# Transposes of one sequence's k and q tiles in one run on TensorE, and a lower rank for the sums of weights, in a scheduled attention and channel-mix kernel

## The chip, the cores and the metric

The kernel runs on one core of a Trainium2 chip. The metric is the device time in microseconds of one execution, median of three runs. TensorE multiplies matrices (PE in the profile; its weight loads have a row of their own, PEld), VectorE is DVE, ScalarE is ACT, GpSimd is POOL, and SyncE (SP) issues most of the DMAs.

## The reference

Eight sequences of 576 tokens, 8 heads of 64, go through an attention by way of 32 packed vectors; what comes out goes, token by token, through a channel mix with a squared relu and a sigmoid gate. All is float32.

```python
def sm_attn(qq, kk, vv):
    s = scale * np.matmul(qq, kk.transpose(0, 1, 3, 2))
    a = np.exp(s - np.max(s, axis=-1, keepdims=True))
    return np.matmul(a / (np.sum(a, axis=-1, keepdims=True) + 1e-09), vv)
p_packed = sm_attn(p, k, v)             # p: 32 vectors a head
x = sm_attn(q, p_packed, p_packed)      # heads side by side: (8, 576, 512)
xk = mu_k * x + (1 - mu_k) * x_prev     # x_prev: x one token earlier
xr = mu_r * x + (1 - mu_r) * x_prev
v = np.maximum(xk @ w_k, 0) ** 2 @ w_v  # w_k 512 x 1024, w_v 1024 x 512
out = v / (1 + np.exp(-(xr @ w_r)))     # w_r 512 x 512
```

## The kernel before

**The channel mix.** The 4608 tokens are cut into nine blocks of 512. Each operand of its matmuls is split into a high and a low part, so that a product is three matmuls of 512 columns (a triple below): `gates` (lines 1209 to 1211, 16 triples a block), `keys` (1160 to 1162, 32 triples) and `values` (1239 to 1241, 32 triples). Seven blocks go that way, and the last two go together as a pair, by a scheme of block products with fewer multiplications (Strassen's) that wants sums of blocks of the weights. Those sums are made by `sums` while blocks 2 to 6 run: adds on VectorE (line 1520), a copy on ScalarE (1496), a subtraction on VectorE (1498), and two stores to DRAM on SP's queue (`far_wr`, `far_wv`, `far_wk`); GpSimd's queue fetches them back for the pair.

**The attention.** A sequence b passes through `front` (scores of the packed vectors, line 670, the softmax `weights_of` with its exponential on line 774, their product with the values, lines 704 or 712), then `back` (scores of q, line 839, softmax, product, line 896). k and q must lie with the head dimension across partitions. For sequences 2 to 7 VectorE transposes them in blocks (line 464), and the softmax weights go to DRAM and back for their own transposition (`far<-at` and `aTd<-far`). The second sequence, b = 1, uses `transposed_on_pe`: its four k tiles and four q tiles, each six pieces of 96 tokens, are transposed on TensorE (line 479) into a PSUM slot of the pool `pa` (two slots) and copied out by ScalarE (line 482). While this happens TensorE also does the gates and keys of block 0, whose inputs come out of `first_mix` (line 1029), through the same two `pa` slots, by way of `first_out` and `first_low` (ScalarE lines 1045 and 1048, VectorE line 1054), and the weights are converted in between (`convert`: lines 299 and 311 on ScalarE, 301, 303 and 313 on VectorE).

**What sets the order.** Every piece of work is a generator that says which engine it wants next and how long that should take. `Flow.run` plays all of them against a clock of its own and emits the instructions in the order in which this planner would start them; on the chip each engine then takes its instructions strictly in that order and waits on semaphores. Of the parts that could start, the planner takes the earliest, and among equals the lowest rank:

```python
part = min(self.parts, key=self.order)
...
return start, part.rank, part.n
```

A part of sequence b ≥ 2 has rank 30 + 0.2 b in `front`, about 29 + 0.2 b in `back`. The sums of weights have `RANK_SUMS`. All names of this paragraph are planning only: no duration of the planner is a time on the chip.

Of the kernel before, what the change touches and what calls it, by code (L numbers as in the profile page):

```python
# [173 lines left out]
def attn_pack_channel_mix(ctx: ExitStack, tc: tile.TileContext, q, k, v, p, mu_k, mu_r, w_k, w_v, w_r, out):  # L174
# [31 lines left out]
    def act(n, after=None, table=None):  # L206
        return "scalar", 0.14 + 0.72e-3 * n, after, table
# [4 lines left out]
    def pe(us, after=None):  # L212
        return "tensor", us, after, None
# [20 lines left out]
    def reached():  # L234

        yield None, 0.0, None, None
# [13 lines left out]
    def tile_(shape, dtype, tag, slot, name=None):  # L250
        return sb.tile(shape, dtype, name=name or tag, tag=f"{tag}{slot}")

    def banks(slot):
        return ps.tile([P, 2, 512], F32, name="pa", tag=f"pa{slot}")
# [71 lines left out]
    def loads(b):  # L326
        flow.spawn(packed(b), lrank(b) - 0.03)
        for src, tag in ((k, "kT"), (v, "vt"), (q, "qT")):
# [8 lines left out]
            for pr in range(NPR):  # L337

                slot = yield from flow.take("raw")
                if b < EARLY:  # L340

                    raw = tile_([P, 6, 2 * D], F32, "raw", slot, "raw")
                    for hh in range(2):
                        yield from load(
                            raw[:T6, :, hh * D:(hh + 1) * D], src[b, 2 * pr + hh].rearrange("(c p) d -> p c d", p=T6),
                            0.5, 0.62,
                        )
                        back_to_issue()
                    flow.spawn(transposed_on_pe(tag, b, pr, slot, raw), rank(b), flow.free["dma"] + LANDS)
                    continue  # L350

                raw = tile_([P, NTB, 32], F32, "raw", slot)
                for o in range(0, P, 32):
                    hh, dh = divmod(o // 32, 2)
                    yield from load(
                        raw[o:o + 32],
                        src[b, 2 * pr + hh, :, 32 * dh:32 * dh + 32].rearrange("(t tb) d -> t tb d", tb=NTB),
                        0.63, 0.41,
                    )
                    back_to_issue()  # L360
                flow.spawn(transposed(tag, b, pr, slot, raw), rank(b), flow.free["dma"] + LANDS)
# [107 lines left out]
    def transposed_on_pe(tag, b, pr, raw_slot, raw):  # L469

        yield from reached()
        kq = yield from flow.take("kq")
        t = tile_([P, S], F32, "kq", kq, tag)
        slot = yield from flow.take("pa")
        pT = banks(slot)
        for hf in range(2):
            yield pe(0.25)
            for c in range(3):
                nc.tensor.transpose(pT[:, hf, c * T6:(c + 1) * T6], raw[:T6, 3 * hf + c], ident[:T6, :T6])
        flow.give("raw", raw_slot)  # L480
        yield act(S)
        nc.scalar.copy(t.rearrange("p (a b) -> p a b", a=2), pT[:, :, :HS])
        flow.give("pa", slot)
        ts[tag, b, pr] = kq, t
        flow.set((tag, b, pr))
# [704 lines left out]
    def gates(i):  # L1190

        for tiles in ((0,), (1, 2, 3)) if i == 0 else ((0, 1), (2, 3)) if i == 1 else ((t,) for t in range(NT)):
            slots, prs = [], []
            if i == 0:
                yield from flow.wait(*made("xr", i, 0, tiles[0]))
                if tiles[0]:
                    flow.keep_busy = 0.0
                    flow.give("m", 3)
            for x in tiles:
                slots.append((yield from flow.take("m")))  # L1200
                prs.append(ps.tile([P, DM], F32, name="pr", tag=f"m{slots[-1]}"))
            for c in range(NC):
                for x, pr in zip(tiles, prs):
                    ts_ = slice(x * P, (x + 1) * P)
                    yield from flow.wait(*made("xr", i, c, x), *(("wr", c, o) for o in range(0, DM, WP)))
                    yield pe(0.685)
                    flow.now.t -= flow.LAG
                    _, xh, xl = xrs[i, c]
                    nc.tensor.matmul(pr, xh[:, ts_], wr_h[:, c, :], start=(c == 0), stop=False)  # L1209
                    nc.tensor.matmul(pr, xh[:, ts_], wr_l[:, c, :], start=False, stop=False)  # L1210
                    nc.tensor.matmul(pr, xl[:, ts_], wr_h[:, c, :], start=False, stop=(c == NC - 1))  # L1211
                    if x == NT - 1:
                        flow.give("sq", xrs.pop((i, c))[0])
            for x, slot, pr in zip(tiles, slots, prs):
                flow.spawn(gated(i, x, slot, pr), 0, flow.t + flow.LAG)
# [50 lines left out]
    def channel_mix():  # L1266
        for i in range(NB - 2):
            if i == 0:
                flow.spawn(first_mix(), RANK_MIX)
            for what, u in SUMS.get(i, ()):  # L1270
                flow.spawn(sums(what, u), RANK_SUMS)
            yield from gates(i)
# [181 lines left out]

    DH = DM // 2
    FORMS = T4, T3, T2, T1
    RANK_SUMS = 20
    SUMS = {
        2: (("wr", 0), ("wr", 1)), 3: (("wv", 0), ("wv", 1)), 4: (("wv", 2), ("wv", 3)), 5: (("wk", 0),), 6: (("wk", 1),),
    }  # L1460
# [583 lines left out]
```

## Time and profile before

| | |
|---|---|
| median of 3 runs (lowest, highest) | 573.69 us (573.64, 574.53) |
| the profiled execution, its own time | 574.06 us |
| its span, first to last instruction | 572.3 us |
| granted TensorE clock, mean | 0.999 |
| TensorE busy | 564.1 us, 99% |
| VectorE busy | 444.5 us, 78% |
| ScalarE busy | 354.0 us, 62% |
| DMA, mean | 136 GB/s |

A busy TensorE is not a TensorE at its peak, since matmuls overlap: a matmul of 512 columns is shown as some 390 ns long, and the next one starts some 230 ns after it. What a wait costs on that engine is therefore read from the distance of the starts, not from the idle time alone.

### The profile page before, as it was taken

The numbers are of one execution on the slowest core, as the hardware profiler recorded it, in microseconds if no ns is written. First come the engines' busy times: TensorE is split into PE (matmuls) and PEld (weight loads), VectorE is DVE, ScalarE is ACT, GpSimd is POOL, SyncE is SP. The second block draws the span as 40 slices with busy tenths as digits, with TensorE's granted clock in tenths as the row PEclk, the third lists the DMA queues.
The fourth block names the chain that finished last, engine by engine and source line by source line (L and its number), as shares of the span: only waits on it lengthen the run. The fifth ranks groups of instructions, "written<-read, shape, count | busy, mean of one in ns | idle before, by whom it ended". The sixth has DMA issues, their size and how long they took to land.

```text
span 572.3 us, 10765 instructions
## 1 busy us (share of the span) xinstructions
PE 564.1 (99%) x4053; PEld 445.1 (78%) x4053; DVE 444.5 (78%) x815; ACT 354.0 (62%) x626; POOL 25.7 (4%) x63
## 2 busy tenths in 40 slices
PE   7999999999999999999999999999999999999997
PEld 7877777887787777778777877787778888888885
DVE  1898897929986888967897789757887579457895
ACT  4789956536924874576545675655678656377840
POOL 3000000000000000000000000000010006300000
PEclk9999999999999999999999999999999999999999
DMA  8979426760768664296339633870045019910026
GB/s 298 390 190 317 95 35 131 152 124 12 153 160 229 133 136 79 97 262 146 56 103 259 144 53 79 190 222 1 1 149 166 0 52 328 296 42 1 0 37 111
DMA packets 188884, 77.66 MB, mean 136 GB/s; under 512 B 152344, under 2 KB 173984, under 8 KB 188576
## 3 DMA queue, kind: packets, MB, share of 16 engines
q1 hardware_dynamic: 182912, 66.35, 44.8%
q0 software_dynamic: 5920, 10.62, 6.5%
q8 instruction: 32, 0.52, 0.4%
q14 instruction: 20, 0.16, 0.1%
HBM read 53.48 MB, written 23.46 MB: 134 GB/s over the span
## 4 chain that ended last, share of the span: by engine, by line
PE 92%; DMA 2%; ACT 2%; DVE 2%; issue 1%; SPq 0%; DVEq 0%; ACTq 0%
PE ph L1160 10%; PE pvo L1239 9%; PE pvo L1240 9%; PE pvo L1241 9%; PE ph L1161 9%; PE ph L1162 9%; PE pr L1209 4%; PE pr L1210 4%; PE pr L1211 4%; PE pa L704 2%; PE pa L896 2%; PE pv L1938 2%; PE pv L1940 2%; PE pv L1939 2%; PE pa L670 1%; DMA q<-in_q 1%
## 5 line engine op out<-in xcount | busy, mean ns | idle before, releaser
L1160 PE MATMUL ph<-xk,wk_h 128*128 128x512 f32 x224 | 90.3, 403 | 0.0
L1239 PE MATMUL pvo<-wv,sq 128*128 128x512 f32 x224 | 89.3, 399 | 0.0
L1161 PE MATMUL ph<-xk,wk_h 128*128 128x512 f32 x224 | 87.4, 390 | 0.0
L1162 PE MATMUL ph<-xk,wk_l 128*128 128x512 f32 x224 | 87.4, 390 | 0.0
L1240 PE MATMUL pvo<-wv,sq 128*128 128x512 f32 x224 | 87.4, 390 | 0.0
L1241 PE MATMUL pvo<-wv,sq 128*128 128x512 f32 x224 | 87.2, 389 | 0.0
L1172 ACT ACTIVATE r<-ph 128x512 f32<-128x512 f32 x56 | 33.5, 600 | 52.0 <-PE ph L1162 51.8
L1239 PEld LDWEIGHTS pvo<-wv,sq 128*128 128x128 f32 x224 | 42.1, 188 | 14.4 <-issue 5.8
L1160 PEld LDWEIGHTS ph<-xk,wk_h 128*128 128x128 f32 x224 | 42.0, 188 | 14.3 <-issue 5.9
L1162 PEld LDWEIGHTS ph<-xk,wk_l 128*128 128x128 f32 x224 | 42.0, 188 | 9.1
L1241 PEld LDWEIGHTS pvo<-wv,sq 128*128 128x128 f32 x224 | 42.1, 188 | 9.0
L1070 ACT COPY xt<-pa 128x576 f32<-128x576 f32 x28 | 30.5, 1177 | 29.7 <-PE pa L896 29.5
L1240 PEld LDWEIGHTS pvo<-wv,sq 128*128 128x128 f32 x224 | 42.1, 188 | 8.0
L1161 PEld LDWEIGHTS ph<-xk,wk_h 128*128 128x128 f32 x224 | 42.1, 188 | 7.7
L1209 PE MATMUL pr<-wr_h,xr 128*128 128x512 f32 x112 | 44.8, 400 | 0.0
L1211 PE MATMUL pr<-wr_h,xr 128*128 128x512 f32 x112 | 43.7, 390 | 0.0
L1210 PE MATMUL pr<-wr_l,xr 128*128 128x512 f32 x112 | 43.7, 390 | 0.0
L1115 DVE SCALAR_TENSOR_TENSOR x<-xt,mus,x 128x128 f32<-128x128 f32 (+5 forms) x88 | 39.8, 494 | 3.9 <-ACT x L1109 3.8
L1183 DVE CAST sq<-r 128x512 fp32r<-128x512 f32 x48 | 20.0, 417 | 29.3 <-ACT r L1175 28.3
L1185 DVE TENSOR_TENSOR sq<-r,sq 128x512 fp32r<-128x512 f32 x56 | 38.1, 681 | 5.6 <-ACT sq L1180 4.6
L1109 ACT ACTIVATE x<-xt,mus 128x128 f32<-128x128 f32 (+5 forms) x88 | 41.3, 515 | 0.7 <-DVE sq L1185 0.7
L1175 ACT ACTIVATE r<-r 128x512 f32<-128x512 f32 x56 | 35.3, 633 | 1.1
(288 smaller groups left out, 1097.5 us busy)
## 6 DMA issues: line engine op xcount, KB each, us to landing
vt<-in_v SPq DMA_DIRECT2D x14, 512.0 KB, 4.6
raw<-in_k SPq DMA_DIRECT2D x96, 72.0 KB, 2.7
raw<-in_q SPq DMA_DIRECT2D x96, 72.0 KB, 2.8
out<-sig SPq DMA_DIRECT2D x23, 256.0 KB, 3.4
st<-in_moe_w_k SPq DMA_DIRECT2D x8, 512.0 KB, 8.6
st<-in_moe_w_v SPq DMA_DIRECT2D x8, 512.0 KB, 6.6
far<-at SPq DMA_DIRECT2D x12, 288.0 KB, 2.7
aTd<-far SPq DMA_DIRECT2D x12, 256.0 KB, 3.1
```

Of the source, the lines that this page charges most:

```text
L1109: nc.scalar.mul(x32[:, o:o + n], xts[b, c][:, 1 + s:1 + s + n], mus[:, j, c:c + 1])
L1115: nc.vector.scalar_tensor_tensor(x32[:, o:o + n], xts[b, c][:, s:s + n], mus[:, j + 1, c:c + 1], x32[:, o:o + n], op0=ALU.mult, op1=ALU.add,)
L1160: nc.tensor.matmul(ph, wk_h[:, c, fs], xh, start=(c == 0), stop=False)
L1161: nc.tensor.matmul(ph, wk_h[:, c, fs], xl, start=False, stop=False)
L1162: nc.tensor.matmul(ph, wk_l[:, c, fs], xh, start=False, stop=(c == NC - 1))
L1185: nc.vector.tensor_tensor(hl[:, 1, :], r, hl[:, 0, :].bitcast(F32), op=ALU.subtract)
L1209: nc.tensor.matmul(pr, xh[:, ts_], wr_h[:, c, :], start=(c == 0), stop=False)
L1210: nc.tensor.matmul(pr, xh[:, ts_], wr_l[:, c, :], start=False, stop=False)
L1211: nc.tensor.matmul(pr, xl[:, ts_], wr_h[:, c, :], start=False, stop=(c == NC - 1))
L1239: nc.tensor.matmul(pv[t], sh, wvs[f][:, 0, :], start=(f == 0), stop=False)
L1240: nc.tensor.matmul(pv[t], sh, wvs[f][:, 1, :], start=False, stop=False)
L1241: nc.tensor.matmul(pv[t], sl, wvs[f][:, 0, :], start=False, stop=(f == NF - 1))
```

## The change

Two edits. In `transposed_on_pe` the request for TensorE is made once for all six pieces of a tile instead of once for each half of three, so that nothing can be put between the halves (and the planner counts 0.45 for the six instead of twice 0.25). And `RANK_SUMS` goes from 20 to 40, from ahead of the attention of sequences 2 to 7 to behind it.

```diff
@@ -473,8 +473,8 @@
         t = tile_([P, S], F32, "kq", kq, tag)
         slot = yield from flow.take("pa")
         pT = banks(slot)
+        yield pe(0.45)
         for hf in range(2):
-            yield pe(0.25)
             for c in range(3):
                 nc.tensor.transpose(pT[:, hf, c * T6:(c + 1) * T6], raw[:T6, 3 * hf + c], ident[:T6, :T6])
         flow.give("raw", raw_slot)
@@ -1454,7 +1454,7 @@
 
     DH = DM // 2
     FORMS = T4, T3, T2, T1
-    RANK_SUMS = 20
+    RANK_SUMS = 40
     SUMS = {
         2: (("wr", 0), ("wr", 1)), 3: (("wv", 0), ("wv", 1)), 4: (("wv", 2), ("wv", 3)), 5: (("wk", 0),), 6: (("wk", 1),),
     }
```

Every engine runs the same instructions as before, but for two loads of ScalarE's function table, of which there are 16 instead of 18. The order is the same, row for row, ahead of the first transposes of sequence 1, and again for all matmuls of the pair at the end; in between it moves on every engine. Triples and the stretches of other work between them keep their number, except that the 48 transposes of line 479 stand in 8 stretches instead of 12. The places of lines 670 to 896 among the triples are the same for sequences 2 and 3 (within five triples), and from 21 triples earlier to 15 later for sequences 4 to 7.

On TensorE, where the gates of block 0 end and its keys begin, before (`raw` is a loaded tile, `pa` the PSUM slot):

```order
L1209 MATMUL pr<-wr_h,xr 128x512
L1210 MATMUL pr<-wr_l,xr 128x512
L1211 MATMUL pr<-wr_h,xr 128x512
L1160 MATMUL ph<-xk,wk_h 128x512
L1161 MATMUL ph<-xk,wk_h 128x512
L1162 MATMUL ph<-xk,wk_l 128x512
L479 MATMUL pa<-ident,raw 128x96 x12
L1160 MATMUL ph<-xk,wk_h 128x512
```

and with the change:

```order
L1209 MATMUL pr<-wr_h,xr 128x512
L1210 MATMUL pr<-wr_l,xr 128x512
L1211 MATMUL pr<-wr_h,xr 128x512
L479 MATMUL pa<-ident,raw 128x96 x6
L1160 MATMUL ph<-xk,wk_h 128x512
L1161 MATMUL ph<-xk,wk_h 128x512
L1162 MATMUL ph<-xk,wk_l 128x512
L479 MATMUL pa<-ident,raw 128x96 x6
```

The second and third k tile, whose halves were mixed into one stretch of twelve, are now two stretches with a triple between them. The same number of triples as before, four, lies between the last matmul of line 1029 and the first of these transposes.

On VectorE, the stretch that ends with the four subtractions that free the two `pa` slots for those transposes (line 1054, 128x320, `xk`), before:

```order
L1054 TENSOR_TENSOR xk<-pa,xk 128x192 x4
L313 TENSOR_TENSOR wk_l<-m,wk_h 128x512 x4
L301 TENSOR_SCALAR m<-m 128x512
L303 SCALAR_TENSOR_TENSOR m<-st,m 128x512
L1054 TENSOR_TENSOR xk<-pa,xk 128x320 x4
```

and with the change:

```order
L524 STREAM_TRANSPOSE pt<-pin 128x128
L1054 TENSOR_TENSOR xk<-pa,xk 128x192 x4
L313 TENSOR_TENSOR wk_l<-m,wk_h 128x512 x3
L301 TENSOR_SCALAR m<-m 128x512
L303 SCALAR_TENSOR_TENSOR m<-st,m 128x512
L301 TENSOR_SCALAR m<-m 128x512
L1054 TENSOR_TENSOR xk<-pa,xk 128x320 x3
L303 SCALAR_TENSOR_TENSOR m<-st,m 128x512
L1054 TENSOR_TENSOR xk<-pa,xk 128x320
```

One subtraction of line 313 has gone behind, one shift of line 301 and, ahead of the first four, the small transpose of line 524 have come in front, and a 303 stands before the last of the four. Between the last line 1054 on `xr` and this place the counts are, before, five 301, five 303 and four 313, and with the change four of each and the 524, up to the third 1054 of 320 columns.

On SP's queue, the loads and stores around the softmax weights of the last sequence (`at` to `far` to `aTd`) and the sums of `w_k`, before:

```order
L221 DMA raw<-in_q 32x18x32 x13
L221 DMA far_wk<-hw 128x2x512
L221 DMA far_wk<-ws 128x2x512
L221 DMA raw<-in_q 32x18x32 x3
L221 DMA far<-at 128x576 x2
L221 DMA aTd<-far 128x4x128
L221 DMA far_wk<-hw 128x2x512
L221 DMA far_wk<-ws 128x2x512
L221 DMA aTd<-far 64x2x32 x2
L221 DMA aTd<-far 128x4x128
L221 DMA aTd<-far 64x2x32 x2
```

and with the change:

```order
L221 DMA raw<-in_q 32x18x32 x16
L221 DMA far<-at 128x576 x2
L221 DMA far_wk<-hw 128x2x512
L221 DMA far_wk<-ws 128x2x512
L221 DMA aTd<-far 128x4x128
L221 DMA aTd<-far 64x2x32 x2
L221 DMA aTd<-far 128x4x128
L221 DMA aTd<-far 64x2x32 x2
L221 DMA far_wk<-hw 128x2x512
L221 DMA far_wk<-ws 128x2x512
```

The first pair of stores has moved from ahead of the last loads of q to behind the stores of the softmax weights, in front of all the loads that bring these back, and the second pair to behind these loads. TensorE's line 704, which reads `aTd`, comes five triples earlier there.

## Rows read from the trace of the kernel before

**Rows 1.** The page, busy time of each engine, share of the span and instructions.

```profile
PE 564.1 (99%) x4053; PEld 445.1 (78%) x4053; DVE 444.5 (78%) x815; ACT 354.0 (62%) x626; POOL 25.7 (4%) x63
```

**Rows 2.** Waits of TensorE, whole span: total, times, longest, in us.

```profile
...
PE pa L479 <- ACT kept L1048: 0.6, 1, 0.6
...
```

**Rows 3.** Timeline from 47 to 52.2: start, us, engine, line, op, count.

```profile
46.90 1.11 ACT L1045 CAST xk<-pa 128x320 fp32r<-128x320 f32 x3
...
48.15 0.48 DVE L1054 TENSOR_TENSOR xk<-pa,xk 128x320 fp32r<-128x320 f32 x1
...
48.67 0.27 ACT L1048 COPY kept<-pa 128x128 f32<-128x128 f32 x1 [0.67 <-DVE xk L1054]
...
49.30 1.31 DVE L1054 TENSOR_TENSOR xk<-pa,xk 128x320 fp32r<-128x320 f32 x3 [0.66 <-ACT xk L1045]
49.39 0.39 PE L1162 MATMUL ph<-xk,wk_l 128*128 128x512 f32 x1
...
50.40 1.25 PE L479 MATMUL pa<-ident,raw 96*128 96x96 f32 x12 [0.62 <-ACT kept L1048]
```

**Rows 4.** Timeline of TensorE: a stretch of three transposes, and one of six.

```profile
53.13 0.39 PE L1161 MATMUL ph<-xk,wk_h 128*128 128x512 f32 x1
53.35 0.39 PE L1162 MATMUL ph<-xk,wk_l 128*128 128x512 f32 x1
53.59 0.41 PE L479 MATMUL pa<-ident,raw 96*128 96x96 f32 x3
...
54.09 0.40 PE L1161 MATMUL ph<-xk,wk_h 128*128 128x512 f32 x1
...
65.07 0.39 PE L1162 MATMUL ph<-xk,wk_l 128*128 128x512 f32 x1
65.31 0.66 PE L479 MATMUL pa<-ident,raw 96*128 96x96 f32 x6
...
66.06 0.40 PE L1161 MATMUL ph<-xk,wk_h 128*128 128x512 f32 x1
```

**Rows 5.** Groups of VectorE by line and shape: busy us, mean ns, idle before.

```profile
L303 DVE SCALAR_TENSOR_TENSOR m<-st,m 128x512 uint32<-128x512 uint32 x20 | 13.8, 690 | 0.5
...
L301 DVE TENSOR_SCALAR m<-m 128x512 uint32<-128x512 uint32 x20 | 8.4, 421 | 3.8 <-ACT m L299 3.7
...
L313 DVE TENSOR_TENSOR wk_l<-m,wk_h 128x512 fp32r<-128x512 f32 x8 | 5.1, 683 | 0.2 <-ACT wk_h L311 0.2
...
L524 DVE STREAM_TRANSPOSE pt<-pin 128x128 f32<-128x128 f32 x7 | 2.1, 307 | 2.1 <-DMA pin<-in_p 2.1
```

**Rows 6.** Groups of ScalarE, same columns.

```profile
L299 ACT ACTIVATE m<-st 128x512 f32<-128x512 f32 x20 | 13.0, 701 | 0.0
L1221 ACT ACT_TABLE_LOAD x9 | 11.5, 1283 | 7.2 <-DMA out<-sig 6.2 <-DVE ws L1520 0.8
...
L311 ACT CAST wk_h<-m 128x512 fp32r<-128x512 f32 x8 | 4.6, 647 | 0.5 <-DVE m L303 0.4
```

**Rows 7.** Timeline around the transpose of the shares (L1980), 38 to 40.

```profile
38.47 0.88 DVE L1054 TENSOR_TENSOR xr<-pa,xr 128x320 fp32r<-128x320 f32 x2
...
39.43 0.22 PE L1980 MATMUL pa<-ident,by_row 8*128 8x8 f32 x1
```

**Rows 8.** Last sequence: timeline of SP's queue, then of TensorE.

```profile
378.24 4.10 SPq L221 DMA_DIRECT2D aTd<-far  x5
...
386.93 0.65 PE L704 MATMUL pa<-vt,aTd 128*32 128x64 f32 x32
```

**Rows 9.** DMA issues by line: count, KB each, median us to landing.

```profile
far_wk<-ws SPq DMA_DIRECT2D x4, 512.0 KB, 3.6
...
aTd<-far SPq DMA_DIRECT2D x24, 16.0 KB, 2.6
```

**Rows 10.** Last store of the sums of w_k (SP), and their first fetch (POOL).

```profile
435.15 0.36 SPq L221 DMA_DIRECT2D far_wk<-ws  x1
...
474.16 0.70 POOL L218 DMA_DIRECT2D wk_h<-far_wk  x1
```

## Prediction

> **What bounds the kernel now.** I read the page first. Its list of busy times gives TensorE 99% of the span, VectorE 78% and ScalarE 62% [rows 1]. A share near 100 does not yet say that the engine never waits, so the second view is the list of TensorE's waits: what ended each stretch in which it had nothing to run. Five waits stand there, and only one of them lies between the first gates of block 0 and the last matmul of the pair: 0.6 us ahead of the transposes of line 479 [rows 2]. Between 51 us and the last matmul that list is empty. So from there on the time is the sum of the distances between the starts of TensorE's instructions, and the two other engines work in its shadow. The third view, the timeline around 50 us, shows the one wait from near, and the reader should follow it by its starts. The last key matmul ahead of it starts at 49.39 and the transposes at 50.40 [rows 3]: 1.01 us. The same pair of instructions a little later, 53.35 and 53.59, is 0.24 apart [rows 4]. The wait thus costs 0.77 us (the 0.6 in the list counts only from the shown end of a matmul that overlaps the next). This is all that a better order can take away here, apart from instructions that TensorE would start closer together.
>
> **The change part by part.**
>
> *Fewer stretches of transposes.* A stretch of other work between triples costs more than its own matmuls, since the triple behind it starts slower. Between the starts of an L1162 and of the second next matmul, an L1161, with nothing in between, lie two distances of 0.22 (53.13 to 53.35 is one), 0.45 in all. With three transposes in between it is 53.35 to 54.09, 0.74: 0.29 more. With six it is 65.07 to 66.06, 0.99: 0.54 more [rows 4]. Two stretches of three cost 0.58, one of six 0.54, so a stretch saved is worth 0.04 us. There are 8 instead of 12: **0.15 us**. The bounds are 0 (read to the hundredth, the difference could be rounding) and 0.3.
>
> *The wait at 50 us.* What ends it? The transposes need a `pa` slot, and both slots hold the last results of line 1029 until ScalarE (1045, 1048) and VectorE (1054) have read them. The list names the copy of line 1048, but the row shows the slower reader: VectorE's first of four subtractions starts at 48.15, ScalarE's copy at 48.67 follows it, the other three take from 49.30 to 50.61, and the transposes start in the middle of these, at 50.40 [rows 3]. So the chain hangs on when VectorE gets to the first one. ScalarE's casts ran from 46.90, so it could have started at about 47.35; VectorE was still busy with weight conversion. With the change VectorE has, up to the third of the four, one 301 and one 303 less and one 524 more: 0.42 + 0.69 - 0.31 = 0.80 us less [rows 5]. ScalarE has one 299 more and one 311 less ahead of its casts, 0.70 - 0.65 = 0.05 more [rows 6], so its casts stay about where they are. The first subtraction then starts at about 47.35, 0.80 earlier, and the three behind it with it: the slot is free at about 49.6 instead of 50.4. TensorE, without a wait, would be ready for the transposes at 49.39 + 0.24 = 49.63. So the first slot comes just in time. The second slot waits for the fourth subtraction, ahead of which a 303 of 0.69 now stands, but in front of its transposes now stands a triple, 0.68 long (three distances of 0.22 to 0.24 [rows 4]). Gain **0.77 us**; bounds 0 (the chain stays late by its whole length) and 0.77.
>
> *What that calls up.* Everything on TensorE between 34 and 50 us that hung on a slot now comes a triple sooner against the other engines. The tightest place is line 1980, which takes its slot from a subtraction of the pair that starts at 38.47 and ran at 39.43 behind four triples [rows 7]; now it runs behind three, so at about 38.75. The first of the pair, 0.48 long, ended by 38.95, but the 313 ahead of it is now a 301, 0.26 shorter [rows 5], so it ends at about 38.7 and TensorE waits **0.1 us**. Bounds 0 and 0.4.
>
> *The rank of the sums.* It moves adds, copies and stores behind the attention of sequences 4 to 7. On TensorE it removes nothing, since there is no wait in that stretch [rows 2]. It adds one only where something comes too late. The sums themselves have time: the last store of `far_wk` is issued at 435.15 and its first fetch at 474.16 [rows 10], 39 us later. The attention gets VectorE earlier, and TensorE's places were moved with it. Taken at **0**, under the cover of triples; if the cover goes, the price is in the rivals. The two table loads that ScalarE saves, 1.28 us each [rows 6], are also taken at 0: no wait of TensorE behind 51 us ends with ScalarE.
>
> **The sum.** 0.77 + 0.15 - 0.10 = 0.82 us. The profiled execution took 574.06 us in all; less 0.82 it is 573.24. It lies 0.37 above the median of the runs, 573.69, and the same sum against the median gives 572.87. I predict **572.9 us**, with 572.4 to 573.6 for this case by the bounds. A measurement of this kernel tells a difference from none at about 0.2%, 1.15 us: this forecast is "no change".
>
> **The rivals.**
>
> *The wait moves.* The slots are two, and behind 55 us the q transposes, the weight transposes (823) and ScalarE's copies take turns on them with little air. TensorE now comes to all of them earlier, while ScalarE does the same work as before. If the freed 0.77 us is given back there, only the stretches are left: 573.69 - 0.15 = 573.5; if the wait stays and 0.4 to 0.8 comes on top, 574.3. For it: the one wait of before is of this kind. Against it: between 55 and 95 us the same traffic caused none.
>
> *The loads of the last softmax weights come late (slower).* On SP's queue two stores of 512 KB, landing 3.6 us after issue, now stand in front of all loads of `aTd`; before, one pair stood behind the first. The last of these loads were issued at 382.3, landed 2.6 later, at 384.9, and line 704 began at 386.93 [rows 8, 9]: 2.0 us of air. TensorE now comes to it five triples earlier, 3.4 us. If the loads are issued when they were, TensorE waits 1.4 us; with one store of 3.6 in front, 5.0. Between these ends, 2.5 us on top of the sum gives 575.4, up to 577.9. It decides from a delay of 2.0 us on. Against it: the stores of the softmax weights are no longer behind a pair of sums and three loads of q, so that all of this starts earlier, by how much no row says.
>
> *ScalarE sets the pace (faster).* If the time went with ScalarE's busy time, two loads less would give 573.69 - 2.57 = 571.1. Against it: 62% busy, and no wait of TensorE ends with it behind 51 us. The Trainium skill has a rule on this side: ScalarE: Activation LUTs, section "Table sets: the hidden batching unit", says to batch activations by table set, and "What ACT_TABLE_LOAD costs" gives some 1283 ns for a load and with its drain 2.66 us a switch, by which the same reasoning would give 568.4, an estimate from that page. The trace agrees on the length of the load, 1283 ns [rows 6], and shows none of these loads under a wait of TensorE.
>
> **How the numbers follow.** The forecast 0.66; the wait moves 0.22; the loads come late 0.09; ScalarE 0.03. The first two lie between 572.3 and 574.6 but for some 0.05 at their ends; the other two fall outside, 0.12. The range is 572.3 to 574.6. Faster than 572.54: ScalarE's case, and the lower end of the forecast when the runs fall well, 0.08, together 0.11. Slower than 574.84: nearly all of the late loads and the upper end of the moved wait, 0.09. The rest, 0.80, is no change.
>
> **What would show it.** In the changed profile the list of TensorE's waits should have no line 479, or one under 0.3; the four subtractions of line 1054 should start near 47.35; the transposes should begin near 49.6 less a triple, 49.0, since one triple has gone behind them; line 1980 should wait 0.1 at most. Behind 55 us the list should stay empty, line 704 of the last sequence included. The busy time of TensorE should hardly move and the span shrink by about 0.8. Wrong would be: a new wait at 823, 712 or 704 that is longer than what line 479 gave back, or a time under 572.3, which would mean that something off TensorE counted that the list of waits does not show.

## The result and the profile after

The changed kernel takes 581.69 us (median of four runs, 580.96 to 582.98), the kernel before, beside it on the same chip, 574.11 us (573.64 to 574.63). The ratio is 1.0138, with an interval of 1.0126 to 1.015: **slower by 7.6 us**. I had predicted 572.9 us, "no change". The profiled execution took 581.53 us with a span of 579.8, which is 7.5 more than before.

The page's busy times of the changed kernel, to be held against [rows 1]:

```profile
PE 567.4 (98%) x4053; PEld 447.0 (77%) x4053; DVE 442.3 (76%) x815; ACT 352.4 (61%) x624; POOL 25.6 (4%) x63
```

They tell little: all shares but GpSimd's have fallen by a point or two, mostly because the span has grown. The list of TensorE's waits, whole span (total, times, longest), tells where to look. Two of its three new rows count here; the third, 0.4 us at line 395, lies in the first 9 us, ahead of anything that the change moves:

```profile
PE pa L896 <- DVE a L886: 2.3, 2, 2.0
PE pa L896 <- DVE e L863: 1.6, 1, 1.6
```

The wait of line 479 [rows 2] is gone. Two long ones and a short one have come, all ahead of line 896, the product of `back`. The two long ones belong to the first half of sequence 5 and of sequence 6.

**The transposes did what was forecast.** Timelines of 36 to 50 us in the changed kernel; the rows of before are [rows 3] and [rows 7]:

```profile
38.34 0.22 PE L1980 MATMUL pa<-ident,by_row 8*128 8x8 f32 x1
...
46.98 0.88 DVE L1054 TENSOR_TENSOR xk<-pa,xk 128x320 fp32r<-128x320 f32 x2
...
48.72 0.69 PE L479 MATMUL pa<-ident,raw 96*128 96x96 f32 x6
```

The first subtraction of line 1054 now starts at 46.98 (forecast: near 47.35), the transposes at 48.72 (49.0). Line 1980 does not wait.

**Place one, sequence 5.** TensorE's timeline of the changed kernel; further down, an undisturbed stretch of line 896 for comparison:

```profile
288.79 0.39 PE L1241 MATMUL pvo<-wv,sq 128*128 128x512 f32 x1
291.21 1.38 PE L896 MATMUL pa<-a,pm 32*64 32x288 f32 x16 [2.03 <-DVE a L886]
292.52 0.67 PE L1239 MATMUL pvo<-wv,sq 128*128 128x512 f32 x1
292.99 0.63 PE L1240 MATMUL pvo<-wv,sq 128*128 128x512 f32 x1
293.42 0.63 PE L1241 MATMUL pvo<-wv,sq 128*128 128x512 f32 x1
...
296.27 0.39 PE L1239 MATMUL pvo<-wv,sq 128*128 128x512 f32 x1
...
301.50 0.39 PE L1211 MATMUL pr<-wr_h,xr 128*128 128x512 f32 x1
301.82 0.74 PE L896 MATMUL pa<-a,pm 32*64 32x288 f32 x16
302.49 0.50 PE L1209 MATMUL pr<-wr_h,xr 128*128 128x512 f32 x1
```

Read it by the starts. From the matmul ahead of line 896 to the one behind it the undisturbed stretch takes 302.49 - 301.50 = 0.99 us; here it takes 292.52 - 288.79 = 3.73, so 2.74 are lost. Of these, 2.10 are the wait (288.79 to 291.21 is 2.42, undisturbed 0.32). The other 0.64 are the product itself: its 16 matmuls take 1.31 to the next start instead of 0.67, although the granted clock is still recorded as 1.00 under them, and why is open. And the loss goes on: the next matmuls stand 0.43 apart instead of 0.23. From 292.52 to 296.27 lie nine distances, 3.75 us; at the usual pace (0.34 behind a stretch, then eight of 0.227) they would take 2.15. That is 1.6 us more, 4.3 in all. The windows of the changed kernel (after the stretch and its length: busy time and instructions of PE, PEld, DVE, ACT, POOL, granted clock, DMA share, GB/s) say why:

```profile
292.00:294.00 2.00, 2.00 (x12) 1.28 (x12) 1.97 (x3) 1.96 (x2) 0.00 (x0) 0.67 0.00 0
294.00:296.00 2.00, 2.00 (x7) 1.54 (x6) 1.33 (x3) 0.84 (x2) 0.00 (x0) 0.50 0.31 65
```

The granted clock, 1.0 through all of this stretch before, falls to 0.50, the level of 1.2 GHz, after TensorE has stood for 2.03 us. The Trainium skill describes this in TensorE: Matmul & The Clock Gate, section "HAM oscillation — how this bites in real kernels": a wait for data between bursts of matmuls can let the clock fall, and the next burst then begins slow. This trace agrees, and shows the price: 1.6 us on top of 2.74.

**Place two, sequence 6**, the same view:

```profile
351.32 0.39 PE L1241 MATMUL pvo<-wv,sq 128*128 128x512 f32 x1
351.64 0.71 PE L896 MATMUL pa<-a,pm 32*64 32x288 f32 x8
354.00 1.16 PE L896 MATMUL pa<-a,pm 32*64 32x288 f32 x8 [1.64 <-DVE e L863]
355.09 0.79 PE L1239 MATMUL pvo<-wv,sq 128*128 128x512 f32 x1
...
357.70 0.39 PE L1239 MATMUL pvo<-wv,sq 128*128 128x512 f32 x1
```

Here the second half of the product waits for its `pa` slot, in which VectorE still reads the scores of the other half of the sequence (line 863). 355.09 - 351.32 = 3.77, less 0.99 is 2.8; the six distances to 357.70 take 2.61 instead of 1.48, 1.1 more. Together 3.9 us. With 0.4 at the short wait near 418 the three places lose 8.6 us, and the transposes give back 1.4 (next section). That leaves 7.2, where the spans differ by 7.5. Not all of these 7.5 belong to the places: the last matmul (line 1893) starts at 574.84 instead of 568.16, 6.7 later, and the other 0.8 arise behind it, where the last stores land. So this sum by rows is about half a microsecond too large. Triples of the same number, compared between the two kernels, settle it: the changed kernel is 1.5 ahead at triple 270, 2.8 behind at 360 and 390, 6.5 behind at 420 and 6.7 from 480 on. Place one thus costs 4.3, place two 3.65 and the short wait 0.2.

**Why VectorE was late.** At both places VectorE is the one waited for, and just ahead of them it is busy without a gap. The windows of the changed kernel show what came before that:

```profile
260.00:270.00 10.00, 10.00 (x144) 7.19 (x143) 1.07 (x2) 2.72 (x5) 0.00 (x0) 1.00 0.69 152
270.00:280.00 10.00, 10.00 (x46) 8.24 (x45) 7.90 (x16) 6.16 (x13) 0.00 (x0) 1.00 0.50 175
280.00:290.00 10.00, 9.18 (x41) 7.27 (x39) 9.97 (x23) 7.03 (x15) 0.20 (x2) 1.00 0.01 2
```

The third pair of numbers is VectorE: 1.07 us of work in the ten from 260 to 270, and then 9.97 of ten. The kernel before had 7.38 there:

```profile
260.00:270.00 10.00, 10.00 (x46) 8.29 (x45) 7.38 (x15) 5.80 (x11) 0.00 (x0) 1.00 0.66 153
```

(The same hole stands at 320 to 330, 2.76 instead of 6.20, ahead of place two.) VectorE's timeline, changed kernel, around the hole:

```profile
247.12 1.22 DVE L1498 TENSOR_TENSOR ws<-ws,hw 128x1024 f32<-128x1024 f32 x1
...
257.19 0.43 DVE L1183 CAST sq<-r 128x512 fp32r<-128x512 f32 x1 [0.32 <-ACT r L1175]
...
266.43 0.29 DVE L727 TENSOR_TENSOR pm<-pa,rs 128x128 f32<-128x128 f32 x1 [7.80 <-PE pa L704]
...
271.17 0.43 DVE L1183 CAST sq<-r 128x512 fp32r<-128x512 f32 x1 [1.57 <-DMA far_wv<-hw]
...
278.95 0.74 DVE L876 TENSOR_REDUCE z<-e 128x18 f32<-128x576 f32 x1
...
288.59 0.16 DVE L878 TENSOR_SCALAR z<-z 128x18 f32<-128x18 f32 x1
...
290.29 0.78 DVE L886 STREAM_TRANSPOSE a<-e 128x576 f32<-128x576 f32 x1
```

The idle time at 266.43 is put down to TensorE's product of line 704, but only because nothing else stood ahead of line 727 in VectorE's order. The row that decides is the one at 271.17. The squares of the keys (lines 1183 and 1185), which had come every few us, stop at 257.19, and the next one waits for a **store of the sums of weights** to land. Both need buffers of the pool `sq`, which by the code has `NF`, eight, of 128x1024. Each part of `sums` takes two of the eight, and two parts run at once; they give them back when their stores have landed. Now SP's queue of the changed kernel, then of the kernel before:

```profile
240.53 11.79 SPq L221 DMA_DIRECT2D raw<-in_q  x16
...
262.79 4.65 SPq L221 DMA_DIRECT2D raw<-in_k  x7
267.48 0.99 SPq L221 DMA_DIRECT2D far_wv<-hw  x1
...
269.98 1.19 SPq L221 DMA_DIRECT2D far_wv<-ws  x1
```

```profile
241.44 0.55 SPq L221 DMA_DIRECT2D far_wv<-hw  x1
...
244.74 0.52 SPq L221 DMA_DIRECT2D far_wv<-ws  x1
```

The last of the data were done at 248.34 (line 1498). The stores were issued from 267.48 to 269.98; before, from 241.44 to 244.74. With rank 40 they stand behind the loads of q, p, k and the softmax weights that this queue issues from 240.53 on. For over 20 us half of the pool is held by finished sums, the squares and behind them the mix of block 4 (lines 1115 and 1137, `xr` in the same pool) pile up, and when the buffers come free all of it has to go through VectorE in front of the softmax of sequence 5: between the starts of lines 876 and 878 of one chain pass 9.6 us, 9.0 of them with mix.

### The profile page after: what moved, and what is told of

Same layout as the page of the kernel before. It is cut to its first block, busy times and chain, and to the rows that moved or that the text cites. A ratio compares the mean times of both kernels' runs of the same rounds, so it can differ in the third digit from the quotient of the medians.

```text
span 579.8 us, 10762 instructions
## 1 busy us (share of the span) xinstructions
PE 567.4 (98%) x4053; PEld 447.0 (77%) x4053; DVE 442.3 (76%) x815; ACT 352.4 (61%) x624; POOL 25.6 (4%) x63
## 4 chain that ended last, share of the span: by engine, by line
PE 76%; DVE 11%; SPq 6%; DMA 4%; ACT 2%; issue 2%; DVEq 0%; ACTq 0%
PE ph L1160 7%; PE ph L1161 7%; PE ph L1162 7%; PE pvo L1239 6%; PE pvo L1240 6%; PE pvo L1241 6%; SPq L221 6%; PE pr L1209 4%; PE pr L1211 4%; PE pr L1210 4%; DVE x L1115 3%; PE pv L1939 2%; PE pv L1938 2%; PE pv L1940 2%; DMA far_wv<-ws 2%
## 5 line engine op out<-in xcount | busy, mean ns | idle before, releaser
L1239 PEld LDWEIGHTS pvo<-wv,sq 128*128 128x128 f32 x224 | 42.8, 191 | 13.6 <-issue 4.9
L1241 PEld LDWEIGHTS pvo<-wv,sq 128*128 128x128 f32 x224 | 42.8, 191 | 9.1
L1240 PEld LDWEIGHTS pvo<-wv,sq 128*128 128x128 f32 x224 | 42.7, 191 | 8.5
L1115 DVE SCALAR_TENSOR_TENSOR x<-xt,mus,x 128x192 f32<-128x192 f32 (+5 forms) x88 | 39.5, 492 | 1.7 <-ACT x L1109 1.7
```

The source lines that it names most:

```text
L1115: nc.vector.scalar_tensor_tensor(x32[:, o:o + n], xts[b, c][:, s:s + n], mus[:, j + 1, c:c + 1], x32[:, o:o + n], op0=ALU.mult, op1=ALU.add,)
L1239: nc.tensor.matmul(pv[t], sh, wvs[f][:, 0, :], start=(f == 0), stop=False)
L1240: nc.tensor.matmul(pv[t], sh, wvs[f][:, 1, :], start=False, stop=False)
L1241: nc.tensor.matmul(pv[t], sl, wvs[f][:, 0, :], start=False, stop=(f == NF - 1))
```

## The experiments

**One edit at a time.** First the merged transposes alone:

```diff
-    RANK_SUMS = 40
+    RANK_SUMS = 20
```

then the rank alone, with the transposes in halves again:

```diff
-        yield pe(0.45)
         for hf in range(2):
+            yield pe(0.25)
```

> Only the first edit: a tile's six transposes in one request, RANK_SUMS back at 20. Theory A (all of the loss comes from the rank of the sums): the attention of sequences 3 to 7 stands at the same triples as in the kernel before, so no wait of line 896 appears, and only the 1.1 to 1.5 us that the same-numbered triples run earlier behind 72 us are left: 572.6 to 573.0 us beside 574.1 of the kernel before. Rival (the merged transposes shift TensorE against VectorE by over a microsecond and that alone makes the products come too early): new waits of line 896 here too, 576 to 582.

> Only the second edit: RANK_SUMS at 40, the transposes in halves as in the kernel before. Theory A: the two long waits of line 896 (sequences 5 and 6) and the two stretches at the 1.2 GHz level are there as with both edits, and the gain of the merged transposes is missing: 581.7 + 1.1 to 1.5 = 582.8 to 583.2 us. Rival (the two edits do it together): at or under 577, with one of the waits gone.

With the transposes alone: 572.47 us (0.1 under what was expected) beside 574.14, ratio 0.997 (0.9958 to 0.9981), span 570.9, no wait of line 479 or 896. With the rank alone: 582.84 us, ratio 1.0143 (1.0117 to 1.0168). The wait of line 479 is there again, and of line 896 these:

```profile
PE pa L896 <- DVE a L886: 2.5, 3, 1.4
...
PE pa L896 <- DVE e L863: 1.9, 1, 1.9
```

In this profiled execution the clock fell at place two alone, where two stretches had been expected. The two edits add up within the spread of the second (580.63 to 584.13): -1.7 and +8.7 us, together +7.0 against the 7.6 measured.

**The price of the clock.** Spare matmuls ahead of the products, so that TensorE has something to run while VectorE is late:

```diff
-        px = [banks(slot) for slot in slots]
+        px = filled([banks(slot) for slot in slots], b)
+    FILL = {5: 19, 6: 15}
+    def filled(px, b):
+        for _ in range(FILL.pop(b, 0)): nc.tensor.matmul(px[0][:, 0, :P], ident, ident, start=True, stop=True)
+        return px
```

> The changed kernel, with 19 and 15 spare matmuls of 128x128 (0.111 us apart) put in front of the first product of line 896 of sequences 5 and 6, where TensorE waited 2.0 and 1.6 us. The result stays the same, as the products overwrite them; TensorE has something to run while it waits for the same VectorE instructions. Theory B (a wait costs its length and, on top, what the clock loses behind it): the granted clock stays at 1.0 behind both places and the time falls by the two slow stretches, 4.33 - 2.1 and 3.6 - 1.65, together 4.2 us: 577.5 us. Rival (the triples behind the waits are slow for another reason, or the clock does not follow the idle time): the stretches at 0.5 stay, 581.7 us.

581.25 us: the expected time was missed, and the rows show why. TensorE in that kernel, place one:

```profile
288.73 4.40 PE L911 MATMUL pa<-ident 128*128 128x128 f32 x38
293.06 0.74 PE L896 MATMUL pa<-a,pm 32*64 32x288 f32 x16
```

19 matmuls of this type stand as 38 records, 0.111 us apart, so that the filling held TensorE for 4.33 us where the wait had been 2.1. The clock did stay at 1.0, but the filling cost as much as wait and clock together. The same with 9 and 7:

> As the earlier run with spare matmuls, but 9 and 7 of them: there each of the 19 and 15 ran as two records of 0.111 us, so that they held TensorE for 4.3 and 3.4 us where the waits were 2.1 and 1.65 us, and this hid what was asked. Now they hold it for 2.0 and 1.55 us. Theory B (a wait costs its length and, on top, what the lower clock behind it costs): the products start about when they did, the granted clock stays at 1.0 behind both, and the time falls by 4.33 - 2.1 and 3.6 - 1.65 us to 577.5 us. Rival (what TensorE runs behind the waits is late for another reason): the time stays at 581 us or over, with new waits behind the two places.

582.62 us: missed again, for a reason of its own. At place one it went as theory B says: the spare matmuls run from 288.89, the product starts at 290.99, and the matmuls behind it are 0.23 apart. At place two TensorE then arrives earlier, VectorE does not, and the wait that it meets there grows to 2.0:

```profile
349.79 1.39 PE L911 MATMUL pa<-ident 128*128 128x128 f32 x11
351.84 0.71 PE L896 MATMUL pa<-a,pm 32*64 32x288 f32 x8 [0.66 <-DVE a L886]
354.59 0.71 PE L896 MATMUL pa<-a,pm 32*64 32x288 f32 x8 [2.04 <-DVE e L863]
```

and the clock falls behind it. What was won at the first place was given back at the second, since VectorE sets the time there. To have one place by itself, the last kernel of this kind fills place two alone (`FILL = {6: 7}`):

> The changed kernel with spare matmuls only at the second place, the first product of sequence 6: 7 of them, 0.22 us each, 1.55 us, where the second half of the products waited 1.64 us. Place one is left as it is, so TensorE comes to place two when it did. Theory B (a wait costs its length and, on top, the lower clock behind it): the wait shrinks to some 0.1 us, the granted clock stays at 1.0 there, and the time falls by 3.6 - 1.65 = about 1.95 us: 579.7 us. Rival (the clock falls there for another reason than TensorE's idle time): the 0.5 stays and so does the time, 581.7 us.

580.21 us (579.17 to 581.29), ratio 1.0113 (1.01 to 1.0126) where the changed kernel had 1.0138 (1.0126 to 1.015): 1.5 us less, with intervals that just touch. TensorE there:

```profile
352.77 1.72 PE L911 MATMUL pa<-ident 128*128 128x128 f32 x14
354.42 1.54 PE L896 MATMUL pa<-a,pm 32*64 32x288 f32 x16
355.90 0.50 PE L1239 MATMUL pvo<-wv,sq 128*128 128x512 f32 x1
356.24 0.40 PE L1240 MATMUL pvo<-wv,sq 128*128 128x512 f32 x1
```

No stretch at the lower clock follows. In this execution, the slowest of its four (581.29), place one waits longer, 2.52 instead of 2.03, which takes back a part. That the clock follows TensorE's standing still at these places is thereby shown: filled, it stays at 1.00 at both (19 and 15) and at place two alone (7). The price on top of the wait, 1.6 and 1.1 us, is read from the rows of the changed kernel.

**The product later.**

```diff
-        flow.now.t += 0.6
+        flow.now.t += 3.2 if b in (5, 6) else 0.6
```

> The changed kernel, with the planner's margin ahead of the product of line 896 raised from 0.6 to 3.2 for sequences 5 and 6 alone, so that these four products stand 4 to 8, 2, 8 triples later or 5 earlier on TensorE (316 becomes 320, 327 becomes 329, 392 becomes 400, 414 becomes 409) while VectorE keeps its work. Theory C (the products were only put too early on TensorE for where VectorE stood): both waits and both stretches at the lower clock are gone, 574.1 - 1.46 = 572.6 us, up to 573.2. Rival (the attention of these sequences as a whole is late, and the wait moves on to the next instruction that needs the slots or the packed values): another line waits 1 us or more, 576 us or more.

578.10 us, ratio 1.0073 (1.0055 to 1.0091): theory C falls, the rival holds. The waits of line 896 are gone and the clock stays at 1.0, but others have come, ahead of the gates, whose PSUM banks and inputs come from VectorE and ScalarE (waits of TensorE, 200 to 400 us):

```profile
PE pr L1209 <- ACT e L874: 1.5, 1, 1.5
PE pr L1209 <- DVE sig L1250: 1.1, 1, 1.1
```

VectorE is late for everything behind the hole, so a later place for these products is no full cure (3.6 us of the 9.2 above the merged transposes alone); the question is what made the hole.

**The stores alone, early.** All of the change stays, but for the rank of the stores:

```diff
-            m = 4 // each
+            m, flow.now.rank = 4 // each, 20
...
-            flow.give("sq", slots[k])
+            flow.give("sq", slots[k]); flow.now.rank = 40
```

> The changed kernel, but each part of the sums asks for its two stores at rank 20 as before and goes back to rank 40 behind them; its adds, copies and subtractions stay at 40. Theory S (the loss is the stores: on SP's queue they stand behind the loads of the next sequence, at 267.5 to 270 us in place of 241.4 to 244.7, and keep four buffers of the pool that the squares of the keys and the mix also need, so that VectorE first idles and then does squares, mix and softmax all at once): the stores of the sums of block 4 are issued a few us behind their last subtraction, VectorE's idle stretch of 7.8 us near 260 is gone, line 896 does not wait, and the time is that of the merged transposes alone, 572.5 us, within 0.5. Rival D (the attention of sequence 5 stands earlier, line 670 at triple 255 in place of 267, and its softmax collides with the mix on VectorE whatever the stores do): waits of line 896 of 1 us or more stay, 576 us or more.

572.89 us, ratio 0.9982 (0.9973 to 0.999), no wait of line 896, no hole. SP's queue and VectorE's share in this kernel:

```profile
248.04 0.57 SPq L221 DMA_DIRECT2D far_wv<-hw  x1
...
253.09 0.46 SPq L221 DMA_DIRECT2D far_wv<-ws  x1
```

```profile
260.00:270.00 10.00, 10.00 (x118) 7.84 (x116) 6.01 (x16) 6.03 (x13) 0.00 (x0) 1.00 0.62 120
```

Sequence 5's attention stands as early as with the change (line 670 at triple 255) and the adds rank as low. Its first product of line 896 stands even earlier, at triple 312 instead of 316. Only the rank of the stores was edited (the rest of the order moves with it), and all of the loss is gone. Theory S stands, rival D falls. That it is the buffers which the late stores keep rests on the row at 271.17 and on the code; a larger pool, or buffers for the sums alone, was not tried.

**The stores alone, late.** The reverse:

```diff
-    RANK_SUMS = 40
+    RANK_SUMS = 20
...
-            m = 4 // each
+            m, flow.now.rank = 4 // each, 40
...
-            flow.give("sq", slots[k])
+            flow.give("sq", slots[k]); flow.now.rank = 20
```

> The reverse: RANK_SUMS at 20, transposes merged, but each part of the sums asks for its stores at rank 40, behind the loads and stores of the attention on SP's queue. Theory S: the loss comes back without the adds having moved behind the attention; TensorE waits at several places behind 200 us and the time is 578 us or more (the changed kernel: 581.7). Rival D: without the lower rank of the adds there is nothing to collide, 572.5 us, within 1.

575.13 us, ratio 1.002 (1.001 to 1.003): 2.7 above the merged transposes alone, where theory S asked for 5.5 or more and rival D for 1 at most, so that both missed. The stores are issued from 272.39 on and the hole is there once (VectorE 1.68 us in 260 to 270); the second set is in time. But the order, in which the planner counts the wait for the stores, here has line 896 of sequence 5 at triple 333 instead of 316, and TensorE waits just once between 200 and 400 us, 0.5 us ahead of line 1209. These rows are of its fastest run (573.92), so most of the 2.7 is not seen in them. Late stores alone cost something, then; that the large part comes when a product stands too early behind the hole is what the next kernel tries.

**Why the product stood there.** The planner counts 0.336 us for 256 columns of line 1115; on the chip four in a row take 1.67, 0.42 each. With the count raised for the mix of blocks 4 and 5 alone:

```diff
-                yield vec(n, after=scaled)
+                yield vec(n + 90 * (i in (4, 5)), after=scaled)
```

> The changed kernel, with the planner's duration of line 1115 raised for blocks 4 and 5 alone: it counts 0.336 us for 256 columns where the trace shows some 0.42 (four in 1.67), and now counts 0.43. The stores stay late and VectorE's idle stretch stays; only the plan knows better when VectorE is done, and puts the products of line 896 of sequences 5 and 6 at triples 318, 328, 397 and 407 in place of 316, 327, 392 and 414. Theory P (late stores make the hole; the planner's short count of the mix then puts the product ahead of VectorE, and this is what turns the hole into waits with a lower clock): the waits of line 896 shrink to under 1 us each, no stretch at 0.5, and the time is 576 to 578 us, like the run with the later product, as VectorE still makes up for the hole and something else waits for it. Rival (the product's place hardly matters, VectorE is late for everything behind the hole): 580 us or more. If the hole itself cost nothing: 572.5.

575.98 us, ratio 1.0043 (1.0023 to 1.0062): 5.7 less than the changed kernel, with the stores as late and the hole as deep (VectorE 1.07 in 260 to 270). Place two no longer waits. Place one still does, longer than expected, but the clock stays:

```profile
291.98 1.38 PE L896 MATMUL pa<-a,pm 32*64 32x288 f32 x16 [1.60 <-DVE a L886]
293.29 0.50 PE L1239 MATMUL pvo<-wv,sq 128*128 128x512 f32 x1
293.63 0.40 PE L1240 MATMUL pvo<-wv,sq 128*128 128x512 f32 x1
```

By this run the loss has two parts: some 3.5 us that stay with the late stores, the hole and the wait at place one (575.98 against 572.47), and 5.7 that a better count takes away. The undercount of line 1115 is not all that puts the product of place one too early, since 1.60 of the 2.03 us of wait remain; what else does was not tried.

**The stores on another queue.** They go out by GpSimd's queue, once with rank 40 for all of `sums`, once with 20 (the 4.0 is what the planner counts until the second store has landed):

```diff
-                    0.46, 1.5,
+                    0.46, 1.5, beside=True,
                 )
-                if not part:
-                    back_to_issue()
+                flow.now.t += 4.0 * part
```

> The changed kernel (RANK_SUMS at 40 for everything, the stores included), but the stores of the sums go out by GpSimd's queue in place of SP's, so that no load of the attention stands in front of them. Theory S (it is the place on SP's queue that holds the buffers of the squares): no idle stretch of VectorE near 260, no wait of line 896, 572.5 us, within 0.5. Rival (it is the rank of the sums as such that makes them late, queue or no queue): waits of TensorE of 1 us or more behind 200 us, 576 us or more.

> RANK_SUMS at 20, transposes merged, the stores of the sums by GpSimd's queue. Theory S: nothing held TensorE behind 55 us with the transposes merged alone, so there is nothing more to win: 572.5 us, within 0.5. Rival (SP's queue is still a cost with the stores early in it, for the loads behind them): under 571.9 us.

575.61 us (1.0037, 1.0023 to 1.0051) and 576.87 us (1.0075, 1.0045 to 1.0105). Both missed. The waits of line 896 shrink to 0.3 and 0.2, as theory S wants, but TensorE now waits for loads. First kernel, then second:

```profile
PE pa L704 <- DMA aTd<-far: 1.0, 2, 0.6
```

```profile
PE pa L670 <- DVE kT L464: 1.7, 1, 1.7
```

In the first the loads of the softmax weights come late, the very mechanism of my rival, at sequence 5 and by stores that run beside the loads instead of queueing in front: SP's 16 loads of q take 14.66 us from 240.66 on, where the changed kernel's took 11.79, and the loads of `aTd` behind them start at 262.00 instead of 258.96. The clock also falls to 0.50 there, from 268 to 271. In the second it is k; its window from 240 to 250 shows a DMA share of 1.08 and TensorE busy for 8.29 of 10. The Trainium skill says in DMA: Bandwidth & Descriptors, section "Issuing engines are not separate DMA queues", that transfers run on the same engines and interleave whichever engine issues them. These two kernels agree: with another queue the stores no longer stand behind the loads, they run against them.

**Two versions beat both kernels:** the merged transposes alone (572.47) and the whole change with early stores (572.89). Their intervals (0.9958 to 0.9981 and 0.9973 to 0.999) overlap, so they are not told apart.

## Why the prediction was wrong

*The wait at 50 us and the stretches of transposes: the mechanism right, the size about half.* Forecast -0.77 - 0.15 + 0.10, -0.82; measured alone -1.7 in the medians, -1.4 in the spans. The chain behaved as worked out from the rows, the wait is gone, line 1980 does not wait, so 0.92 was to be had. Of the rest, 0.3 arise ahead of the first gate matmul (line 1209), where nothing was changed; the 0.2 that remain are not explained.

*The wait moves, ScalarE's pace:* neither. Between 51 and 200 us TensorE is busy throughout, and two table loads less bought nothing that shows.

*Late loads of `aTd`:* not in this kernel; line 704 of the last sequence stands in no list of waits. I had the right queue and looked at the wrong side of it. I asked what comes late when stores stand in front of loads, and the order had also put stores behind loads.

*The rank of the sums, "taken at 0": this is the step that failed.* Alone it cost 8.7 us, and by another way than any rival named; all that is slower than 574.84 had been given 0.09. Its reasoning was: no wait in that stretch, the sums have 39 us until they are fetched, and "the attention gets VectorE earlier, and TensorE's places were moved with it". Each half fell:

- "The sums themselves have time" is true of their **results**. It says nothing of the **buffers** that they hold until the stores have landed, and these are half of the pool that the squares and the mix need. A lower rank for a part that already holds buffers holds up the parts that rank ahead of it. The rows were within reach: the order of SP's queue showed stores moving behind loads, and the code shows whose buffers they read.
- "TensorE's places were moved with it" took the planner's word for when VectorE would be done. Where VectorE has slack, an undercount of 0.08 us in an operation does no harm; in the pile behind the hole, where it ran 9.97 us of 10, the undercounts of 16 operations on 256 columns add up to 1.3 us, and the product waits. That is a part only: with the count raised, 1.60 us of wait stayed at place one.

*The price of a wait.* I priced every wait at its length. Behind the two long ones the clock fell, which cost 1.6 and 1.1 us more.

## What to carry to other kernels

When work is given a lower priority, list what it holds while it waits (buffers, banks, places on a queue) and who needs that; the deadline of its result is the smaller question. In an order fixed ahead of time, a store's place on its queue decides when its buffer comes back: here data done at 248.34 were issued from 267.48 on. And a full TensorE hides a late engine only as long as that engine has gaps: look for holes in its windows, not at its mean share, which here fell by a mere two points.

## What was not expected of the hardware

How the clock answers to a wait is not a matter of its length alone in these rows. It fell to 0.50 after waits of 2.03 and 1.64 us (changed kernel), 1.9 (rank alone), 2.04 (9 and 7 spare matmuls) and 2.52 (7 at place two alone, at its place one). It stayed at 1.00 after 1.4 (rank alone), 1.47 and 1.13 (product later), 1.60 (mix as measured) and 1.71 (stores by GpSimd at rank 20, ahead of line 670). And in the kernel with the stores on GpSimd's queue at rank 40 it stood at 0.50 from 268 to 271, behind two waits of 0.55 and 0.45 between the short matmuls of line 704. What sorts these cases was not tried.

Nor does the recorded clock tell all of the price: behind waits of 2.03, 1.60 and 1.4 us the 16 matmuls of line 896 took 1.31 us to the next start instead of 0.67, with the clock recorded as 1.00 under them.

A matmul of 128x128 by the identity in this type stands in the trace as two records 0.111 us apart; taking a record for an instruction made the first filling twice as long as meant.
